# Moving query transposes later in the step and taking extra keys and queries out through the segment's key buffer

## The chip, the cores and the metric

The kernel runs on one core of one Trainium2 chip. The metric is the device time of one execution in microseconds (us), and less is better. The kernel before takes a median of 1097.09 us in three runs (1093.23 to 1100.27). Every run carries the mean clock that was granted to TensorE; a run is called slow when it is over 1.5% above the fastest of the same kernel, and fast otherwise.

## The reference, cut to what matters

The first half is a recurrent attention: 64 segments of 32 tokens each, one after the other, because every segment reads eight memory rows that the segment before it wrote. The second half is a gated feed-forward part; the change does not touch it.

```python
B, S, Dm = (1, 2048, 640);  H, Dh = (32, 128);  M, seg = (8, 32)
for s in range(n_seg):                               # 64 segments, strictly in order
    xs = x[:, s * seg_len:(s + 1) * seg_len, :]
    h = jnp.concatenate([mem, xs], axis=1)           # 8 memory rows + 32 tokens
    q, k, v = h @ Wq, h @ Wk, h @ Wv                 # einsum per head, 32 heads of 128
    p = softmax(mask(q @ k.T * scale))
    o = einsum('bhte,hed->btd', p @ v, Wo)
    mem = o[:, :M, :].copy()                         # the next segment starts from this
    outs.append(o[:, M:, :])
h  = x + concatenate(outs)
h2 = h + feed_forward(layernorm(h))
```

## The kernel before

A **step** is one segment. The columns of a projection that the eight memory rows leave free are used for 24 tokens of later segments, called **riders**. Four steps carry 96 riders; the other 32 tokens of a block of 128 are the **extra** tokens, and they get a projection of their own in three pieces: keys in a third step (`s % 4 == 2`), queries in a fourth step (`s % 4 == 3`), values in the next first step.

A projection lands in PSUM, VectorE and ScalarE cast it into `tok` (four tiles of 128x512, two halves: 0 and 1 for keys, 2 and 3 for queries), and a DMA transpose turns a half into the layout that the scores need. All transposes are issued by SyncE (SP), and the program gives each engine one list of instructions, in the order in which they are recorded. TensorE's part of a step is, in order: the **score block**, the **memory product** (probabilities of the memory rows times the values), the transposing of its result, the **output product**, the **rider product** (`pv_x`), the projections of the next keys and queries, and the **memory pick** (the next memory queries, read straight from `tok`). An **eviction** is the cast of a projection out of PSUM. The helper `add(engine, f, r=, w=)` records an instruction with the keys that it reads and writes, and the waits follow from those keys.

```python
def to_tok(b, t, eng):                               # PSUM bank b -> tok[t]
    copy_op(eng, tok[t][:, :], bank(b), [B(b)], [("tok", t)])

def pick_mem(bk):                                    # L453: memory queries by TensorE, straight from tok
    ...
    add("pe", f, r=[("tok", 2), ("tok", 3), ("ident",)], w=[B(bk)])

def trans_q(after=()):                               # QS <- tok[2,3], DMA transpose, 256 KB
    dma_t(QS[...], tokp[1][:, :], [("tok", 2), ("tok", 3)] + list(after), [("QS",)])

def scores(s):                                       # L572
    ...
    add("pe", f, r=[("KS",), ("Kr", q), ("Qm", q), ("Qr", q)], w=[B(P0), B(P1)])

def extra_units(s):
    ...
    j = (1, 0, 2)[r]                                 # keys, queries, values
    def evac():
        for i, e in enumerate(("act", "act")):
            if j == 2: to_v(BQ[i], Vr[q], i, ("Vr", q), e)
            else:      to_tok(BQ[i], 2 + i, e)       # extra keys and queries: into tok[2,3]
        if j == 1:
            dma_t(Kr[q][...], tokp[1][:, :], [("tok", 2), ("tok", 3)], [("Kr", q)])
    def fin():                                       # extra queries: tok -> QS -> Qr
        trans_q()
        late_q.append(lambda: evac_q(QS, ("QS",), t0, 32, 0, "act"))
    return part, evac, (fin if j == 0 else None)

for s in range(NSEG):
    ...                                              # key projection
    to_tok(BQ[0], 0, "act"); to_tok(BQ[1], 1, "dve")
    dma_t(KS[...], tokp[0][:, :], [("tok", 0), ("tok", 1)], [("KS",)])   # keys of this segment
    trans_ox()
    project(a, ks, 0, (0, 1), (P0, P1), spare=40)    # query projection
    to_tok(P0, 2, "act"); to_tok(P1, 3, "dve")
    for f in late_k + late_q: f()
    qlate = nr and s % 4 < 2
    if nr and not qlate and s < NSEG - 2:
        trans_q()                                    # third and fourth steps: at once
    project(...)                                     # values, first part
    pick_mem(T0)                                     # L453
    ...                                              # values, second part
    scores(s); exp_mem(); exp_x()                    # L572
    if nr:
        v_riders(t0, nr, (), ...)                    # riders' values: Vr <- Vp, plain DMA from POOL
        if s < NSEG - 2 and not qlate:
            evac_q(QS, ("QS",), t0, nr, M, "act")    # QS -> Qr
    ...                                              # extra projection in pieces, memory product (L609)
    if evac: evac()
    wo_pass(T1, ...)                                 # output product (L644)
    ...
    pv_x(s, P0)                                      # rider product (L690)
    if nfin: nfin()
```

The softmax here doesn't subtract the row's maximum and nothing guards it: scores larger than these inputs give would overflow.

## Time and profile before

| | before |
|---|---|
| time, median of 3 | 1097.09 us |
| span and granted clock of the profiled run | 1095.7 us, 0.997 |
| mean step, first / second / third / fourth | 13.39 / 13.64 / 13.51 / 13.47 us |
| TensorE waits for a query eviction at the memory pick | 0.9 us, once |

A step is measured from the start of one score block to the start of the next, over the third to the sixtieth-second segment (15 steps of each kind). What the trace says of the tile QS, of which the last line gives the time from the issue of a transpose into it to its landing:

```profile
DMA to landing us min/median/max: 3.0/3.1/4.9
```

Where QS is transposed early or late in a step, 256 KB take about 3.1 us.

### The profile page before, as it was taken

To read this page: it belongs to the slowest core of one execution; us is meant where nothing else is said; L and a number is where in the kernel's file an instruction comes from. 1 tells how busy PE (TensorE), PEld (TensorE's weight loads), DVE (VectorE), ACT (ScalarE), POOL (GpSimd) and SP (SyncE) were. 2 spreads that over 40 slices of the span, in tenths; PEclk is the share of its full clock that TensorE was granted. 3 is DMA by queue.
4 is the path that set the end of the run, shared out by engine and by line. 5 is a ranking of instruction groups with operands and counts; after the bars stand their busy time and mean duration, and the time that the engine had idled before them with its cause. 6 is when DMAs were issued, how large, how long until landed. Compare 5 with 4: busy or idle time off the path is not lost.

```text
span 1095.7 us, 55782 instructions
## 1 busy us (share of the span) xinstructions
PE 1054.8 (96%) x27875; PEld 517.3 (47%) x23292; DVE 608.8 (56%) x1673; ACT 362.6 (33%) x792; POOL 260.0 (24%) x521
## 2 busy tenths in 40 slices
PE   4689999999999999999999999999999999999999
PEld 2344545454545454544454544454545465444444
DVE  3245656565656565666666666565656554553532
ACT  1214343333333333333333333333333322231211
POOL 1013232323223232323232323232323243000000
PEclk9999999999999999999999999999999999999999
DMA  9946464546454654556566666554555448122100
GB/s 363 387 101 106 89 107 90 102 89 104 90 98 95 102 94 97 94 114 108 112 113 112 110 109 109 100 97 95 95 94 93 92 118 288 45 78 74 29 19 25
DMA packets 285371, 121.61 MB, mean 111 GB/s; under 512 B 260880, under 2 KB 274788, under 8 KB 285136
## 3 DMA queue, kind: packets, MB, share of 16 engines
q1 hardware_dynamic: 267456, 95.52, 41.9%
q0 software_dynamic: 17264, 22.26, 8.8%
q8 instruction: 201, 3.29, 1.3%
q14 instruction: 34, 0.28, 0.1%
q10 hardware_dynamic: 416, 0.26, 0.1%
HBM read 36.79 MB, written 7.19 MB: 40 GB/s over the span
## 4 chain that ended last, share of the span: by engine, by line
PE 91%; DMA 5%; SPq 3%; DVE 1%; issue 1%; ACT 0%; DVEq 0%
PE ps L422 25%; PE ps L400 24%; PE ps L644 13%; PE ps L1051 11%; PE ps L690 3%; PE ps L666 3%; PE ps L572 3%; SPq L360 3%; DMA Wo<-in_A_Wo_dram 3%; PE ps L1092 3%; PE ps L609 2%; DMA KS<-tok 2%; PE ps L453 2%; PE ps L624 1%; DMA Kr<-tok 1%
## 5 line engine op out<-in xcount | busy, mean ns | idle before, releaser
L422 PE MATMUL ps<-W,act_r 128*32 128x512 bf16 x4292 | 406.5, 384 | 6.8 <-DMA W<-in_A_Wv_dram 2.6
L400 PE MATMUL ps<-W,act_r 128*32 128x512 bf16 x3588 | 362.4, 379 | 0.0
L422 PEld LDWEIGHTS ps<-W,act_r 128*32 128x32 bf16 x4292 | 132.1, 97 | 250.4 <-issue 151.3
L360 POOL DMA_DIRECT2D Vr<-Vp x312 | 156.1, 508 | 345.9 <-ACT Px L591 274.0
L464 ACT ACTIVATE tok<-ps 128x512 bf16<-128x512 f32 x192 | 110.9, 593 | 229.0 <-PE ps L400 200.2
L644 PE MATMUL ps<-Wo,oT 128*32 128x160 bf16 x8064 | 156.9, 234 | 8.7 <-DMA Wo<-in_A_Wo_dram 4.8
L466 DVE CAST tok<-ps 128x512 bf16<-128x512 f32 x131 | 90.6, 691 | 129.6 <-PE ps L400 109.8
L644 PEld LDWEIGHTS ps<-Wo,oT 128*32 128x32 bf16 x8064 | 142.8, 97 | 30.3 <-DVE oT L466 16.2
L422 PE MATMUL ps<-W,act_e 128*32 128x512 bf16 x900 | 89.3, 381 | 0.0
L400 PE MATMUL ps<-W,act_e 128*32 128x512 bf16 x900 | 88.9, 379 | 0.0
L555 DVE STREAM_TRANSPOSE TBf<-ps 128x64 f32<-128x64 f32 (+1 forms) x128 | 33.6, 263 | 95.8 <-PE ps L644 95.7
L360 POOL DMA_DIRECT2D attn_d<-wtok x62 | 46.4, 748 | 161.0 <-ACT wtok L464 161.0
L705 DVE TENSOR_TENSOR ox<-ps,rx 128x512 bf16<-128x512 f32 x128 | 82.5, 686 | 2.2
L464 ACT ACTIVATE Qr<-QS 128x512 bf16<-128x512 bf16 (+3 forms) x107 | 69.7, 680 | 35.9 <-DMA QS<-tok 35.9
L464 ACT ACTIVATE Vp<-ps 128x256 bf16<-128x256 f32 (+1 forms) x126 | 48.5, 385 | 81.5 <-PE ps L400 79.0
L1066 DVE TENSOR_TENSOR hT<-g,ps 128x512 bf16<-128x512 bf16 (+1 forms) x56 | 38.5, 688 | 47.2 <-PE ps L1051 43.4
L1051 PE MATMUL ps<-xn2T,Wg 128*128 128x512 bf16 x260 | 64.6, 379 | 0.0
L1051 PE MATMUL ps<-xn2T,Wu 128*128 128x512 bf16 x260 | 64.6, 379 | 0.0
L1064 ACT ACTIVATE g<-ps 128x512 bf16<-128x512 f32 (+1 forms) x56 | 32.4, 592 | 91.6 <-PE ps L1051 91.6
L466 DVE CAST Vp<-ps 128x512 bf16<-128x512 f32 x64 | 44.2, 691 | 28.4 <-PE ps L400 22.9
L464 ACT ACTIVATE wtok<-ps 128x160 bf16<-128x160 f32 x62 | 18.8, 303 | 117.0 <-DVE TBf L555 117.0
L1092 PE MATMUL ps<-Wd,hT 128*128 128x320 bf16 x210 | 57.2, 299 | 0.0
(121 smaller groups left out, 1190.7 us busy)
## 6 DMA issues: line engine op xcount, KB each, us to landing
Vr<-Vp POOLq DMA_DIRECT2D x124, 48.8 KB, 2.0
W<-in_A_Wk_dram SPq DMA_DIRECT2D x2, 2560.0 KB, 13.4
W<-in_A_Wq_dram SPq DMA_DIRECT2D x2, 2560.0 KB, 23.1
W<-in_A_Wv_dram SPq DMA_DIRECT2D x2, 2560.0 KB, 27.7
Wo<-in_A_Wo_dram SPq DMA_DIRECT2D x2, 2560.0 KB, 28.5
xt<-in_A_x_dram SPq DMA_DIRECT2D x30, 160.0 KB, 2.7
Vr<-Vp POOLq DMA_DIRECT2D x96, 32.5 KB, 2.1
at<-attn_d SPq DMA_DIRECT2D x16, 160.0 KB, 3.7
```

The lines of the kernel that those rows point to most:

```text
L360: add(eng, lambda e: e.dma_start(dst, src), r=r, w=w, dma=True)
L400: return pe.add_instruction(mybir.InstMatmult(name=nc.get_next_instruction_name(), engine=mybir.EngineType.PE, ins=[pe.lower_ap(rhs), pe.l ...
L422: ins = pe.matmul(*a, start=(c == 0), stop=(c == DC - 1), skip_group_check=True)
L464: add("act", lambda a: a.activation(dst, src, ACTF.Copy), r=r, w=w)
L466: add("dve", lambda v: v.tensor_copy(dst, src), r=r, w=w)
L555: add("dve", lambda v, lo=lo, hi=hi: v.transpose(TBf[:, lo:hi, :].rearrange("p c t -> p (c t)"), src[:, 32 * lo:32 * hi]), r=[wkey], w=[(" ...
L572: i = pe.matmul(bank((P0, P1)[g % 2])[p:p + (M if a else 32), 40 * k:40 * k + 40], lh, Qr[:, h, q, :], start=True, stop=True, skip_group_c ...
L644: i = pe.matmul(bank(bk)[32 * gg:32 * gg + 32, 0:160], src[:, hb, :], w[:, gg], start=(hb == ORDER[0]), stop=(hb == ORDER[31]), skip_group ...
L705: add("dve", lambda v, kh=kh: v.tensor_tensor(ox[:, :, kh, :], src[:, :, kh, 0:128], ap(rx, kh, [[2, 4], [0, 128]]), ALU.mult), r=[B(b0 + ...
L1051: ins = pe.matmul(bank(bk), w[:, c, lo:lo + 128], xn2T[par][:, :, c, :], start=(c == 0), stop=(c == DC - 1))
L1066: add("dve", lambda v: v.tensor_tensor(hT[par][lo:128, j, :], g1[gi][lo:128, :], bank(bu)[lo:128, :], ALU.mult), r=[B(bu), ("g1", gi)], w= ...
L1092: i = pe.matmul(*a, start=(j == 0), stop=(j == FC - 1), skip_group_check=True)
```

## The change

The intent has two halves. The transpose of the own queries in third and fourth steps was issued just before the scores; moved behind the memory probabilities, it should no longer disturb the instruction fetch of TensorE. And the extra keys and queries, which went through the query half of `tok` and QS, leave through KS, which is idle between the scores and the next segment's keys.

```diff
+    def evac_qx(src, t0):                     # half by VectorE, half by ScalarE: tok -> Qr
+        for n, eng in enumerate(("dve", "act")):
+            for q, o, m, lo in pieces(t0, SEG, 0):
+                copy_op(eng, Qr[:, 16 * n:16 * n + 16, q, ...], src[:, 16 * n:16 * n + 16, lo:lo + m],
+                        [("tok", 2 + n)], [("Qr", q)])
 ... exp_mem:
-                r=[("om",), ("mbd",)], w=[("Pbd", i)])
+                r=[("om",), ("mbd",)], w=[("Pbd", i), ("qgo", i)])
 ... extra_units, evac and fin:
+                elif True:
+                    copy_op(e, KS[...][:, 512 * i:512 * i + 512], bank(BQ[i]), [B(BQ[i])], [("KS",)])
-                dma_t(Kr[q][...], tokp[1][:, :], [("tok", 2), ("tok", 3)], [("Kr", q)])
+                dma_t(Kr[q][...], KS[...], [("KS",)], [("Kr", q)])
-            trans_q()
-            late_q.append(lambda: evac_q(QS, ("QS",), t0, 32, 0, "act"))
+            dma_t(tokp[1][...], KS[...], [("KS",)], [("tok", 2), ("tok", 3)])
+            late_x.append(lambda: evac_qx(tokp[1][...], t0))
 ... loop, after the key evictions (so ahead of the query evictions):
+            for f in late_x:
+                f()
-            if nr and not qlate and s < NSEG - 2:
+            qmid = nr and s % 4 >= 2 and s < NSEG - 2
+            if nr and not qlate and not qmid and s < NSEG - 2:
                 trans_q()
 ... after v_riders:
-                if s < NSEG - 2 and not qlate:
+                if qmid:
+                    trans_q([("qgo", 1)])
+                if s < NSEG - 2 and not qlate and not qmid:
                     evac_q(QS, ("QS",), t0, nr, M, "act")
 ... end of the step:
+            if s > 0 and qmid:
+                late_k.append(lambda t0=t0, nr=nr: evac_q(QS, ("QS",), t0, nr, M, "act"))
```

More of the change, by code (lines that the diff above doesn't have):

```diff
@@ L487, in evac_q @@
             copy_op(eng, Qr[:, :, q, M + o:M + o + m], src[:, :, lo:lo + m], [skey], [("Qr", q)])
+    def evac_qx(src, t0):
+        for n, eng in enumerate(("dve", "act")):
+            for q, o, m, lo in pieces(t0, SEG, 0):
+                copy_op(eng, Qr[:, 16 * n:16 * n + 16, q, M + o:M + o + m], src[:, 16 * n:16 * n + 16, lo:lo + m],
+                        [("tok", 2 + n)], [("Qr", q)])
     def seg_slot(s):
@@ L877, in evac @@
                     to_v(BQ[i], Vr[q], i, ("Vr", q), e)
+                elif True:
+                    copy_op(e, KS[:].rearrange("p h t -> p (h t)")[:, 512 * i:512 * i + 512], bank(BQ[i]), [B(BQ[i])], [("KS",)])
                 else:
@@ L880, in evac @@
             if j == 1:
-                dma_t(Kr[q][:].rearrange("p h t -> p (h t)").rearrange("p (k r) -> p k r", r=128), tokp[1][:, :],
-                      [("tok", 2), ("tok", 3)], [("Kr", q)])
+                dma_t(Kr[q][:].rearrange("p h t -> p (h t)").rearrange("p (k r) -> p k r", r=128),
+                      KS[:].rearrange("p h t -> p (h t)"), [("KS",)], [("Kr", q)])
         def fin():
-            trans_q()
-            late_q.append(lambda: evac_q(QS, ("QS",), t0, 32, 0, "act"))
+            dma_t(tokp[1].rearrange("p (k r) -> p k r", r=128), KS[:].rearrange("p h t -> p (h t)"), [("KS",)],
+                  [("tok", 2), ("tok", 3)])
+            late_x.append(lambda: evac_qx(tokp[1].rearrange("p (h t) -> p h t", t=SEG), t0))
         return part, evac, (fin if j == 0 else None)
@@ L902, in woe_store @@
                 w=[("attne", b, dg)], eng="pool")
-    late, late_q, late_k = [], [], []
+    late, late_q, late_k, late_x = [], [], [], []
     for s in range(NSEG):
@@ L933, in build_kernel @@
             to_tok(BQ[1], 1, "dve")
+            for f in late_x:
+                f()
+            late_x = []
             if last:
```

## The prediction

> **What bounds the kernel now.** I read the page's busy shares first, then the chain that ended last, then TensorE's waits, then the timeline of one group of steps. Two parts of the page and the waits view:
>
> ```profile
> PE 1054.8 (96%) x27875; PEld 517.3 (47%) x23292; DVE 608.8 (56%) x1673; ACT 362.6 (33%) x792; POOL 260.0 (24%) x521
> ...
> PE 91%; DMA 5%; SPq 3%; DVE 1%; issue 1%; ACT 0%; DVEq 0%
> ...
> PE ps L644 <- issue: 2.6, 8, 0.9
> PE ps L572 <- DMA KS<-tok: 1.6, 5, 0.6
> PE ps L453 <- DVE tok L466: 0.9, 1, 0.9
> ```
>
> TensorE is busy 96% of the span and carries 91% of the chain; the DMA and SP-queue shares of the chain are mostly the opening load of weights (until 58 us). Every wait that the view names inside the 64-step loop is small. Only what shortens TensorE's own idle time counts, so I measured each step as the distance between the starts of two score blocks (L572, 64 of them in the trace). Steps come in fours. From the third to the sixtieth the means are 13.39, 13.64, 13.51 and 13.47 us for first, second, third and fourth step, and the cleanest steps take 13.23. Cutting each step at score block, memory product (L609), output product (L644), rider product (L690) and memory pick (L453), and subtracting the near-shortest value of the same piece, leaves an excess of about 18 us in the loop. About 12 us of it lies in third and fourth steps:
> - L644, output product: 6.0 us in third and fourth steps against 1.8 us in first and second.
> - score block to memory product: 2.7 us against 0.2 us (1.57 us in most of these steps, 1.43 in the others).
> - two single stalls, 0.95 and 0.48 us.
>
> The L644 loss looks so in the chain in order of time (start, length, what); a whole block is one line of 128, a broken one is two with nothing named between:
>
> ```profile
> 720.49 2.21 PE ps L644 x128
> ...
> 747.24 1.20 PE ps L644 x66
> 748.44 0.88 issue
> 749.31 1.28 PE ps L644 x62
> ```
>
> TensorE waits for no tile there. The break falls where a 16 KB packet of the instruction queue is due. In the packet records this packet starts a median 1.50 and 1.59 us after the scores in first and second steps, but 1.96 and 2.16 us in third and fourth, where a QS transpose, issued 0.2 to 1.2 us before the scores, is still moving data (its packets come some 1.3 us after the issue). In the worst step it started at 2.46 us, took 1.73 us, and L644 lost 1.11 us.
>
> The SP queue and ScalarE in a third step (scores at 621.28 us):
>
> ```profile
> 620.44 1.23 SPq L363 DMA_TRANSPOSE QS<-tok  x1
> 624.48 0.94 ACT L464 ACTIVATE Qr<-QS 128x512 bf16<-128x512 bf16 x2 [1.26 <-DMA QS<-tok]
> 625.32 1.06 ACT L464 ACTIVATE tok<-ps 128x512 bf16<-128x512 f32 x2
> 626.47 2.25 SPq L363 DMA_TRANSPOSE Kr<-tok  x1
> 629.17 1.21 SPq L363 DMA_TRANSPOSE at<-xt  x1
> 630.71 2.50 SPq L363 DMA_TRANSPOSE KS<-tok  x1
> 633.09 0.60 ACT L464 ACTIVATE tok<-ps 128x512 bf16<-128x512 f32 x1 [2.50 <-DMA Kr<-tok]
> ```
>
> The reader is to see two things: the extra keys leave late, because ScalarE first waits for QS and copies it; and the next queries' eviction waits 2.50 us for the slow Kr transpose, since both use the same half of tok. That became the 0.95 us stall, and it happened once in 15.
>
> **What the Trainium skill says.** "Perfetto Trace Analysis", Identifying the Most-Contended Engine, warns that matmul busy time is no measure of distance to the roofline; so I use step lengths, not the 96%. "Runtime: NRT & Kernel Launch", Instruction fetch mechanics, says instructions come in 16 KiB blocks of 256 over a DMA queue of the sequencer's own, mostly hidden. The trace agrees on the size (three 16,384-byte packets a step) and, in these steps, not on "hidden". "DMA: Bandwidth & Descriptors", Queues, rings and completion order, says each DMA engine changes between queues after each packet. If so a fetch should slip in among the transpose's packets; that it starts 0.5 us later where one is in flight speaks for more delay than that. The same page, Issuing engines are not separate DMA queues, says all issuers share the 16 DMA engines: moving a transpose moves load, it removes none.
>
> **The change part by part.**
> 1. *Own queries of third and fourth steps* (30 transposes): the QS transpose waits for the second half of the memory probabilities, 1.4 to 1.5 us after the scores start instead of 0.2 to 1.2 us before. Its packets then come at about 1.5 + 1.3 = 2.8 us and end near 4.3, after the fetch at 1.4 to 2.4. L644 should then lose what it loses in first and second steps: 6.0 - 1.8 = 4.2 us gained. The delay of the first memory wait, seen with QS in flight and in no first or second step, should go: 2.7 - 0.2 = 2.5 us. Of both I expect some two thirds, as other traffic (riders, stores) stays: 6.7 x 0.65 = 4.4 us.
> 2. *The copy QS to Qr* goes to the next step, behind its first query eviction. ScalarE (33% busy) loses no time on the path; first and second steps work so already, finishing before their scores.
> 3. *Extra keys (third step)* leave PSUM into KS: the same two 0.59 us ScalarE copies, no longer behind QS or tok. Their transposes start about 4.7 us after the scores as in the best steps, not at 5.2, 6.1 and 6.4 as in three of them. The tok wait goes, worth the two single stalls: 1.4 us at most; I take 1.0.
> 4. *The new wait.* KS is also where the next step's keys land, so their transpose must wait until Kr has been read out. Kr is issued at 4.7 and lands in 4.7 to 5.4 us (page: 5.2 median), so at 9.4 to 10.1; the KS transpose is issued at 9.45 today. It lands 3.1 to 3.5 us later and the scores begin at 13.24, so there are about 13.24 - 9.45 - 3.3 = 0.5 us of slack. A mean delay of 0.4 us mostly fits in; I take 0.15 us lost in each of 15 third steps: 2.2 us.
> 5. *Another new wait in the same place*: the attention store issued from the POOL queue at the start of a third step was made to read KS only for ordering; ScalarE must now await its landing before it writes KS. It lands at 3.8 to 4.6 us today and the extra projection ends at 3.4. Without the QS transpose in flight I expect it sooner: the one such store with no QS in flight (near the end of the loop) landed in 2.3 us. So about 3.1 us, no cost; this is the shakiest step.
> 6. *Extra queries (fourth step)* go KS, then tok, then half by VectorE and half by ScalarE into Qr (a 0.3 us and a 0.6 us copy) instead of one 1.05 us ScalarE copy. The transpose from 4.6 lands in 3.7 to 4.2 us, before the KS transpose at 9.45. Off the path: 0.
>
> The compiled TensorE order is the same but for one added wait in the score blocks. Sum: -4.4 - 1.0 + 2.2 = -3.2 us, so about **1094 us**.
>
> **The rivals.**
> - *KS becomes the wait.* If the store still lands at 4.2 us, the key copies end at 5.4, Kr lands at 10.5, KS is issued at 10.6 and lands at 13.9: 0.6 us lost in 14 third steps, 8 us, which eats all gains and gives about 1100 us; with Kr slowed further by QS and riders (they now share 2.8 to 5 us) 1.0 us a step, 1106 us. For it: Kr took 6.6 us once, and KS landings of 4.2 us occur where another transpose was issued just ahead. Against: the slack of 0.5 us.
> - *Fetch delay was not QS.* Second steps lose L644 time too (1.4 us) with no such transpose at that moment. Then only 1.0 us is gained and 2.2 lost: 1098 us.
> - *Everything works.* All 6.7 + 1.4 us gained, no KS wait: 1089 us.
> - *TensorE stays the bound whatever happens.* Even without any loss in third and fourth steps the gain is 12 us, 1.1%; a 2% gain is out of reach, and a 2% loss needs 0.7 us in each of the 30 changed steps.
>
> **Range and chances.** The middle of the working is 1094; the rivals span 1089 to 1106, and the runs of before spread 1093.2 to 1100.3. I take 1085 to 1104. Faster by over 2% 0.01, slower by over 2% 0.02, within 2% 0.97.
>
> **What would show it.** Right if in third and fourth steps the instruction packet starts near 1.5 us and L644 runs unbroken; if ScalarE's waits for QS (35.9 us, 30 times) vanish; if VectorE and ScalarE never wait for Kr before tok; and if the third step's KS transpose is issued by 10 us with TensorE's waits on KS (1.6 us, 5 times) little changed. Wrong if waits of L572 on KS grow to 10 us or more (part 4 or 5), if the key copies start near 4.3 us (part 5), or if the L644 breaks stay (part 1).

## The result, and the profile after

The changed kernel takes a median of **1125.01 us** in four runs (1123.30 to 1128.42); the kernel before took 1095.91 us beside it, also in four. The ratio is **1.0265** (95% interval 1.0222 to 1.0309). A ratio here is always the mean time of one kernel's fast runs over the mean of the other's fast runs of the same rounds, so it is not quite the quotient of the medians. The prediction had put 0.02 on such an outcome.

Lines moved by six in the middle of the file: the scores are now L578, the memory product L615, the output product L650, the rider product L696. The page's busy shares and chain of the kernel after:

```profile
PE 1061.9 (95%) x27875; PEld 521.0 (46%) x23292; DVE 612.4 (55%) x1688; ACT 357.4 (32%) x792; POOL 260.1 (23%) x521
...
PE 81%; DMA 12%; SPq 3%; DVE 2%; issue 1%; ACT 1%; DVEq 0%
```

TensorE has the same number of instructions and is busy 95% of the span, so the first line shows hardly anything. The second does: TensorE's share of the chain fell from 91% to 81%, and DMA's rose from 5% to 12%. TensorE's own waits and the queue's waits (engine, line, what was waited for: us in total, times, longest) say where:

```profile
PE ps L453 <- DVE tok L466: 21.2, 14, 3.3
...
PE ps L422 <- issue: 3.8, 10, 0.8
...
PE ps L578 <- DMA KS<-tok: 2.1, 5, 0.7
```

```profile
SPq L166 <- DMA QS<-tok: 54.7, 15, 4.4
...
SPq L166 <- DMA tok<-KS: 42.8, 14, 4.2
```

The wait for KS, which the prediction had feared most, is still small. The memory pick of L453 waits 21.2 us for the query eviction, 14 times; before it was 0.9 us, once. Fourteen times in 15 blocks of four is a per-block effect. The steps show which:

| mean us of a piece | score block to memory product | to transposing its result | to output product | output product | rider product to pick | pick to next scores | step |
|---|---|---|---|---|---|---|---|
| third, before | 1.55 | 1.24 | 0.57 | 2.45 | 6.08 | 1.63 | 13.51 |
| third, after | 1.43 | 1.24 | 0.57 | 2.33 | 6.22 | 1.70 | 13.48 |
| fourth, before | 1.49 | 1.24 | 0.57 | 2.61 | 5.96 | 1.60 | 13.47 |
| fourth, after | 1.42 | 1.24 | 0.57 | 2.33 | 7.62 | 1.86 | 15.03 |

Times 15, the fourth steps cost 23.4 us more, third steps 0.4 us less, first steps 0.2 us less and second steps 1.4 us more. The profiled spans differ by 25.9 us; nearly all of the rest lies in the second segment, which is 1.6 us longer (14.73 us against 13.11). That is not the change's: the trace after has an interval of half clock there, at 72 us, and the trace before has none; of the runs below, third_only and no_riders4 have such an interval too and take 14.85 and 14.73 us, fourth_only has none there and takes 13.21. Within the fourth steps the parts that the change aimed at did get shorter (1.1 and 4.3 us), and the stretch from the rider product to the pick got 24.9 us longer.

Here is one fourth step of the kernel after (scores at 428.64, the next at 443.39), the chain in order of time: start, length, what.

```profile
430.24 5.20 DMA QS<-tok
...
435.50 4.45 DMA tok<-KS
...
439.98 0.30 DVE Qr L466
...
440.31 0.64 ACT Qr L464
...
441.04 0.70 DVE tok L466
441.74 0.05 issue
441.79 0.36 PE ps L453 x8
```

Five links follow each other without a gap. The own queries' transpose, issued 1.60 us after the scores, reads `tok[2,3]`. The extra queries' transpose *writes* `tok[2,3]` and so cannot be issued before the first has landed. Its result must be copied out of `tok` before the next queries can be cast into it. VectorE copies first, then ScalarE (both write the same key of Qr), and only then may VectorE cast the queries into the tile that ScalarE has just read. The memory pick ends the chain. The same step in the timelines of SP, POOL and VectorE:

```profile
430.24 1.53 SPq L363 DMA_TRANSPOSE QS<-tok  x1
435.50 1.23 SPq L363 DMA_TRANSPOSE tok<-KS  x1
440.03 1.23 SPq L363 DMA_TRANSPOSE KS<-tok  x1
```

```profile
430.55 2.00 POOL L360 DMA_DIRECT2D Vr<-Vp  x4 [1.25 <-ACT Px L597]
```

```profile
439.98 0.29 DVE L466 COPY Qr<-tok 128x512 bf16<-128x512 bf16 x1 [2.06 <-DMA tok<-KS]
441.04 0.69 DVE L466 CAST tok<-ps 128x512 bf16<-128x512 f32 x1 [0.77 <-ACT Qr L464]
```

The reader is to see the POOL line: the rider stores are issued from 0.3 us after the QS transpose on, and QS takes 5.2 us instead of 3.1. The tile view of QS, whose last line before read 3.0/3.1/4.9, has a new maximum; its median hides the matter because first and second steps are unchanged:

```profile
DMA to landing us min/median/max: 3.1/3.1/6.5
```

Over the 15 fourth steps `tok<-KS` is issued a median 6.66 us after the scores (5.30 to 8.38). The key transpose of the next segment, which shares the SP queue, moves with it, from a median 9.58 to 11.39 us.

One small part of the loss is of another kind. The granted clock of the profiled run is 0.989 against 0.997, and all four runs after have 0.988 to 0.992. From the third to the sixty-second segment the trace has three intervals of 3.4 us at half clock (332, 554 and 670 us), each within 1 us after one of the long waits at L453; the trace before has none there. The Trainium skill, "TensorE: Matmul & The Clock Gate", Part 1: The HAM clock gate, gives the idle state half the clock and a window of about 3.4 us, and the trace agrees with both figures. If all work in these intervals ran at half speed they cost at most 3 x 1.7 = 5 us (an estimate), already contained in the step lengths above. They come after the waits, and they are not the main loss: the trace of fourth_only below has only one of them and the same long fourth steps (14.96 us).

### The profile page after: what moved, and what is told of

Same layout as the page of the kernel before. It is cut to its first block, busy times and chain, and to the rows that moved or that the text cites. A ratio compares the mean times of both kernels' runs of the same rounds, so it can differ in the third digit from the quotient of the medians.

```text
span 1121.6 us, 55749 instructions
## 1 busy us (share of the span) xinstructions
PE 1061.9 (95%) x27875; PEld 521.0 (46%) x23292; DVE 612.4 (55%) x1688; ACT 357.4 (32%) x792; POOL 260.1 (23%) x521
## 4 chain that ended last, share of the span: by engine, by line
PE 81%; DMA 12%; SPq 3%; DVE 2%; issue 1%; ACT 1%; DVEq 0%
PE ps L422 22%; PE ps L400 20%; PE ps L650 12%; PE ps L1068 10%; DMA tok<-KS 5%; PE ps L672 3%; PE ps L578 3%; PE ps L696 3%; SPq L360 3%; DMA Wo<-in_A_Wo_dram 3%; PE ps L1109 3%; DMA QS<-tok 2%; PE ps L615 2%; DMA KS<-tok 2%; PE ps L453 2%; PE ps L630 1%
## 5 line engine op out<-in xcount | busy, mean ns | idle before, releaser
L422 PE MATMUL ps<-W,act_r 128*32 128x512 bf16 x4292 | 413.2, 387 | 9.2 <-issue 3.8
L400 PE MATMUL ps<-W,act_r 128*32 128x512 bf16 x3588 | 366.3, 381 | 0.0
L650 PE MATMUL ps<-Wo,oT 128*32 128x160 bf16 x8064 | 156.3, 236 | 4.2 <-DMA Wo<-in_A_Wo_dram 3.1
L650 PEld LDWEIGHTS ps<-Wo,oT 128*32 128x32 bf16 x8064 | 144.9, 98 | 22.9 <-DVE oT L466 16.8
L464 ACT ACTIVATE tok<-ps 128x512 bf16<-128x512 f32 x132 | 78.3, 593 | 201.1 <-PE ps L400 176.5
L400 PE MATMUL ps<-Wd,hT 128*128 128x320 bf16 x210 | 57.2, 299 | 0.0
L1109 PE MATMUL ps<-Wd,hT 128*128 128x320 bf16 x210 | 57.2, 299 | 0.0
```

The lines of the kernel that those rows point to most:

```text
L400: return pe.add_instruction(mybir.InstMatmult(name=nc.get_next_instruction_name(), engine=mybir.EngineType.PE, ins=[pe.lower_ap(rhs), pe.l ...
L422: ins = pe.matmul(*a, start=(c == 0), stop=(c == DC - 1), skip_group_check=True)
L464: add("act", lambda a: a.activation(dst, src, ACTF.Copy), r=r, w=w)
L650: i = pe.matmul(bank(bk)[32 * gg:32 * gg + 32, 0:160], src[:, hb, :], w[:, gg], start=(hb == ORDER[0]), stop=(hb == ORDER[31]), skip_group ...
L1109: i = pe.matmul(*a, start=(j == 0), stop=(j == FC - 1), skip_group_check=True)
```

## The experiments

The theory after the first look: fourth steps lose because the query half of `tok` is still tied up when the next queries arrive. It needs three things together: **(a)** the extra queries are transposed into the tile that the late QS transpose still reads, **(b)** that transpose is slowed by the rider stores, **(c)** the copies stand ahead of the query evictions. The rivals: the loss comes from KS and the third steps (the prediction's own rival), or merely from later transposes sharing DMA with more traffic. Twelve kernels were run in five batches. Ratios are against the kernel before in the same batch. Labels of edits are relative to the kernel after.

### One half of the change at a time

**third_only** keeps the third step's half; **fourth_only** the fourth step's; **own_early4** keeps all of the change but leaves the own queries' transpose of fourth steps at its old place.

```diff
 third_only
-                elif True:
+                elif j == 1:
-            dma_t(tokp[1][...], KS[...], ...); late_x.append(...)
+            trans_q()
+            late_q.append(lambda: evac_q(QS, ("QS",), t0, 32, 0, "act"))
-            qmid = nr and s % 4 >= 2 and s < NSEG - 2
+            qmid = nr and s % 4 == 2 and s < NSEG - 2
 fourth_only
-                elif True:
+                elif j == 0:
-                      KS[...], [("KS",)], [("Kr", q)])
+                      tokp[1][:, :], [("tok", 2), ("tok", 3)], [("Kr", q)])
-            qmid = nr and s % 4 >= 2 and s < NSEG - 2
+            qmid = nr and s % 4 == 3 and s < NSEG - 2
 own_early4
-            if nr and not qlate and not qmid and s < NSEG - 2:
+            if nr and not qlate and s < NSEG - 2 and (not qmid or s % 4 == 3):
-                if qmid:
+                if qmid and s % 4 != 3:
```

> Only the third step's parts of the change: its own queries late, its extra keys through KS; the fourth step as in the kernel before. Theory (the whole loss is in the fourth step): third steps about 13.5 us, fourth 13.5 us, time 1093 to 1098 us, the same as before. Rival (the keys' buffer KS, with the store that reads it, is the wait): 1108 us or more.

> Only the fourth step's parts; the third step as in the kernel before. Theory: the loss is all here, 1118 to 1126 us, TensorE waits at L453 about 20 us. Rival (the two steps' parts need one another, or the third carries it): under 1108 us.

> The changed kernel, but in fourth steps alone the own queries' QS transpose starts at its old place (before the scores); the extra queries still go KS, tok, Qr. Theory (the late QS transpose holds the tok half, so the extra queries' transpose starts at 6.5 to 8.4 us instead of 4.6): tok<-KS is issued near 4.7 us after the scores and lands by 9.5, TensorE's waits at L453 fall from 21.2 us to under 4, the fourth step falls from 15.0 to about 13.5 us, time about 1101 us. Rival (the detour through KS and tok is itself too long, or VectorE's place in its queue): fourth step stays over 14.3 us, time over 1112 us.

Measured, against 1097.78 us before: third_only 1094.78 us, ratio 0.9996 (0.9952 to 1.0040); fourth_only 1123.22 us, 1.0233 (1.0192 to 1.0275); own_early4 1097.13 us, 1.0003 (0.9981 to 1.0024). The wait at the memory pick in their traces, in this order:

```profile
PE ps L453 <- DVE tok L466: 0.9, 1, 0.9
```

```profile
PE ps L453 <- DVE tok L466: 22.2, 14, 3.2
```

```profile
PE ps L453 <- DVE tok L466: 0.3, 1, 0.3
```

The loss and the wait are in the fourth step's half alone. The rival of the prediction, a loss through KS in third steps, falls: third_only has the new KS route for the keys and costs nothing. And own_early4 narrows it further. It still takes the extra queries by KS and `tok`, with the same copies ahead of the evictions; only the own queries' transpose is early again. One step of it (scores at 417.19) has the extra transpose issued 4.78 us after the scores:

```profile
416.71 1.26 SPq L363 DMA_TRANSPOSE QS<-tok  x1
421.97 1.24 SPq L363 DMA_TRANSPOSE tok<-KS  x1
```

So neither the KS detour nor the copies hurt by themselves. The later QS transpose does; that it does so through `tok` is shown by own_buffer below.

### The rider stores

**no_riders4** leaves the rider stores out in fourth steps. That gives wrong values; the comparison with the reference was within tolerance all the same, so it is no proof of correctness. **riders_after4** keeps them but lets them wait until QS has landed.

```diff
 no_riders4
-                v_riders(t0, nr, (), ...)
+                if s % 4 != 3:
+                    v_riders(t0, nr, (), ...)
 riders_after4
-                v_riders(t0, nr, (), ...)
-                if qmid:
+                if qmid and s % 4 == 3:
+                    trans_q([("qgo", 1)])
+                v_riders(t0, nr, [("QS",)] if qmid and s % 4 == 3 else (), ...)
+                if qmid and s % 4 != 3:
                     trans_q([("qgo", 1)])
```

> The changed kernel without the rider stores Vr<-Vp of fourth steps (wrong values on purpose). If those stores slow the QS transpose: it lands in about 3.2 us (at 4.8 after the scores) instead of 4.9 to 5.8, tok<-KS is issued near 4.9, fourth step about 13.5 us, time about 1101 us. If they do not: QS lands as late as now, tok<-KS at 6.5 or later, time 1118 us or more.

> The changed kernel, but in fourth steps the rider stores wait until the QS transpose has landed; all values right. Theory (riders beside QS are what makes it late): QS lands in 3.3 us, tok<-KS is issued near 4.8 but now shares with the riders and lands in 4 to 5 us, at 9 to 9.8; fourth step 13.3 to 13.9 us, time 1094 to 1105 us. Rival (the extra transpose, now beside the riders, is slowed as QS was): fourth step over 14.3 us, over 1112 us.

Measured: no_riders4 1096.28 us, 0.9992 (0.9957 to 1.0028), against 1097.78. QS lands in about 3.3 us. One step (scores at 416.13) on SP:

```profile
417.73 1.23 SPq L363 DMA_TRANSPOSE QS<-tok  x1
420.87 1.70 SPq L363 DMA_TRANSPOSE tok<-KS  x1
...
425.43 1.23 SPq L363 DMA_TRANSPOSE KS<-tok  x1
```

QS is issued 1.60 us after the scores exactly as in the kernel after, and yet the next transpose follows 3.14 us later instead of 5.26. That is link (b). (The edit also shortens the second transpose, from a median 4.2 to 3.1 us in the four landings that each trace has; riders_after4 below relieves QS alone.) The fourth step falls to 13.16 us, 0.31 below before: this is what the change's gain looks like undisturbed. Part of it returns elsewhere: the scores wait for KS 7.4 us, 11 times, most of it (4.5 us) at the end of third steps, which are the same code as in the kernel after but 13.74 us long here.

riders_after4: 1104.29 us against 1098.15, 1.0040 (0.9997 to 1.0082). QS lands in 3.45 us and `tok<-KS` is issued at 4.75 us, both as wanted, but now the riders meet the second transpose, which takes a median 5.25 us instead of 4.2 (four landings each):

```profile
PE ps L453 <- DVE tok L466: 6.8, 9, 1.6
```

Two thirds of the wait are gone and one third stays: the traffic was moved, not removed.

### A buffer of their own for the extra queries

There were 1564 free bytes per partition. A 2 KB buffer XS fits if it shares 512 bytes with a tile that is used in second steps only. **own_buffer** lets the extra queries go KS -> XS -> Qr, with the copies where they were; **own_buffer_late** also puts the copies behind the query evictions.

```diff
 own_buffer
+    XS = ar.alloc("XS", [128, H, SEG], BF16)      # its last 512 bytes are oTn's
-            dma_t(tokp[1][...], KS[...], [("KS",)], [("tok", 2), ("tok", 3)])
-            late_x.append(lambda: evac_qx(tokp[1][...], t0))
+            dma_t(XS[...], KS[...], [("KS",)], [("oTn",)])
+            late_x.append(lambda: evac_qx(XS, t0))
 own_buffer_late, further
-            for f in late_x:
-                f()
-            late_x = []
-            for f in late_k + late_q:
+            for f in late_x + late_k + late_q:
```

> The changed kernel, but the extra queries' transpose writes a buffer of its own (XS, sharing 512 bytes with oTn, which no fourth step uses) instead of the tok half; QS still starts late and the riders still slow it. Theory (it is the wait for tok, behind the slowed QS, that costs): XS<-KS is issued near 4.7 us, fourth step 13.3 to 13.7 us, time 1093 to 1102 us. Rival (the late, slowed QS delays whatever follows it in the DMA queues, tok or not): XS lands after 10 us, fourth step over 14.2 us, time over 1110 us.

> As own_buffer, and the two copies XS to Qr stand behind the next queries' evictions instead of ahead of them. If part of the loss is the place in VectorE's and ScalarE's queues: a few tenths of a us less in the fourth step than own_buffer, 1092 to 1098 us. If the place costs nothing once XS lands by 9.4 us: equal to own_buffer within 0.3%. If ScalarE now fills up before the scores: the first step 0.2 to 0.4 us longer, 3 to 6 us more.

Measured against 1098.15: own_buffer 1099.69 us, 1.0017 (0.9985 to 1.0049); own_buffer_late 1097.67 us, 1.0001 (0.9968 to 1.0034). Both traces have no wait at the pick worth naming. QS is as late as in the kernel after and slower still (6.4 to 8.5 us in the three landings that each trace has), and the rider stores are all there; only the collision on `tok` is gone, and with it the whole loss. That settles link (a). Link (c) is worth little once (a) is gone: the two fourth steps are 13.54 and 13.53 us long.

But own_buffer_late should have been *faster* than before, since the output product is whole (2.33 us) and nothing waits. The gain went into the next piece: rider product to pick takes 6.34 us in fourth steps against 5.96 before, and TensorE's waits show an unnamed one inside the projections:

```profile
PE ps L423 <- issue: 3.8, 9, 1.1
```

In the packet records the second 16 KB instruction packet of these steps starts a mean 6.02 us after the scores, 0.46 us after the rider product starts. Before it started at 5.91 us, but there the rider product starts later too, at the same 5.91 us. Over the 15 fourth steps of this run, the packet's start correlates at 0.95, its end at 0.97, with the length of the piece from rider product to pick. It looks as if, in place of the first packet of the step, the second is now delayed.

### Is it the traffic at the second packet?

**both_own_buffer** takes the extra keys through XS as well. **buffer_no_riders** is own_buffer_late without rider stores in third and fourth steps (wrong values). **buffer_riders_after** is own_buffer_late with the riders behind QS in fourth steps.

```diff
 both_own_buffer
-                    copy_op(e, KS[...], bank(BQ[i]), [B(BQ[i])], [("KS",)])
+                    d, k = (XS, "oTn") if j == 1 else (KS, "KS")
+                    copy_op(e, d[...], bank(BQ[i]), [B(BQ[i])], [(k,)])
-                      KS[...], [("KS",)], [("Kr", q)])
+                      XS[...], [("oTn",)], [("Kr", q)])
 buffer_no_riders
-                v_riders(t0, nr, (), ...)
+                if s % 4 < 2:
+                    v_riders(t0, nr, (), ...)
 buffer_riders_after: as riders_after4
```

> As own_buffer_late, and the third step's extra keys are also staged in XS, so neither the next keys' transpose nor the attention store holds them. Theory: nothing of the change's new waits is left and its gains at L644 (about 6 us) and at the first memory wait (about 2 us) remain: third steps 13.3, fourth 13.2 to 13.4 us, 1087 to 1093 us, faster than both kernels by 0.4 to 0.8% over before. Rival (the gains return as waits elsewhere): 1095 us or more.

> own_buffer_late without the rider stores of third and fourth steps (wrong values on purpose). Question: own_buffer_late takes the tok wait away and L650 stays unbroken, yet it only equals the kernel before; its rider-product-to-pick piece is 0.10 us longer in third and 0.38 us longer in fourth steps than in the kernel before, with the second instruction packet late. Theory (QS, slowed by the riders, is now beside that second packet): the packet starts by 5.2 us on average, that piece is 5.93 to 6.0 us in both steps, third steps about 13.3 and fourth about 13.2 us, time 1085 to 1092 us. Rival (the extra transposes themselves delay the packet): the piece stays over 6.15 us, time 1094 us or more.

> own_buffer_late, and in fourth steps the riders wait until QS has landed (right values): a try at a version that beats both kernels. Theory: fourth steps lose the second-packet delay, 13.2 to 13.35 us instead of 13.53, time 1090 to 1095 us, 0.2 to 0.6% under the kernel before. Rival (the riders now stand beside the extra queries' transpose and delay it or the next keys): fourth step 13.5 us or more, 1097 us or more, nothing won.

both_own_buffer: 1099.81 us against 1098.15, 1.0021 (0.9995 to 1.0047). This missed what I expected of it (1087 to 1093). Its fourth step is better (13.25), but its third step, where the keys are now issued without waiting for the store, is worse: 13.70 us, with 6.51 us from rider product to pick. The unnamed wait grew rather than went:

```profile
PE ps L423 <- issue: 5.2, 11, 0.9
```

buffer_no_riders: 1090.78 us against 1100.41, **0.9901** (0.9867 to 0.9935). Third and fourth steps are 13.18 and 13.12 us long, the piece is 5.94 and 5.93, the second packet starts at a mean 5.26 us in fourth steps, and the unnamed wait is down to

```profile
PE ps L423 <- issue: 1.6, 5, 0.5
```

This is the only kernel that beat the one before clear of noise, by 1%, and it does so by leaving out work. It shows that, with the tile collision gone, the rest of the expected gain is held back where rider stores and transposes move together. That they do it by delaying the instruction packet is what the packet starts (6.02 against 5.26) and the correlation suggest; no run held up a packet by anything else.

buffer_riders_after: 1099.10 us against 1100.41, 1.0006 (0.9974 to 1.0037). The piece is 5.93 us and the packet starts at 5.27 us, as without riders. But XS<-KS, now beside the riders, lands at a median 9.86 us (four landings), and the key transpose may not write KS before KS has been read out. It is issued at a median 10.46 us instead of 9.30 in own_buffer_late. This is the prediction's rival "KS becomes the wait", only in the fourth step. The queue's wait and TensorE's:

```profile
SPq L166 <- DMA XS<-KS: 48.3, 14, 4.0
```

```profile
PE ps L579 <- DMA KS<-tok: 9.4, 16, 1.3
```

In own_buffer_late the queue waited so for 18.9 us, 5 times. From pick to scores the fourth step takes 2.19 us instead of 1.63. The traffic came back as another wait and nothing was won.

### The copies, and a second way to hold tok

**uncrossed** asks how much of the loss is the crossing of the copies: ScalarE casts the next queries into `tok[2]` and VectorE into `tok[3]`, but VectorE copies out of 2 and ScalarE out of 3, one after the other. The edit gives each engine the tile that it fills next, and a key of Qr of its own. The copies also name their tile of `tok` as written, which keeps the following cast behind them.

```diff
-        for n, eng in enumerate(("dve", "act")):
+        for n, eng in enumerate(("act", "dve")):
-                        [("tok", 2 + n)], [("Qr", q)])
+                        [("tok", 2 + n)], [(("Qr", "Qx")[n], q), ("tok", 2 + n)])
 scores:
-        add("pe", f, r=[("KS",), ("Kr", q), ("Qm", q), ("Qr", q)], ...)
+        add("pe", f, r=[("KS",), ("Kr", q), ("Qm", q), ("Qr", q), ("Qx", q)], ...)
```

> The changed kernel, but each engine copies out the quarter of tok that it fills next, and the two copies no longer wait for one another: in the changed kernel VectorE's 0.29 us copy, ScalarE's 0.63 us copy and VectorE's 0.69 us eviction follow one another, 1.8 us from landing to pick; here the longer of 0.63 + 0.60 and 0.29 + 0.69, about 1.3 us. Theory (the rest of the loss is the late landing): fourth steps 0.5 us shorter, about 14.5 us, time 1114 to 1119 us. Rival (the copies' order is what costs): under 1106 us. Rival (it hides under something else): 1122 us or more.

Its four runs are 1124.61 (slow state), 1105.14, 1116.25 and 1117.35 us; the three fast ones give 1.0160 (1.0101 to 1.0220) against 1095.89 before, with the verdict "unclear". Against the 1.0265 of the kernel after this suggests some 11 us saved of 29 ((1.0265 - 1.0160) x 1096), but the runs scatter by 12 us and were not taken in the same rounds as the kernel after. It is a hint that link (c) takes a share as long as (a) stands, no more.

**own_queries_last** was meant as a version that wins: own_buffer_late, with the own queries' transpose of fourth steps issued behind the extra queries' one, out of the way of both packets.

```diff
-                if qmid:
+                if qmid and s % 4 != 3:
                     trans_q([("qgo", 1)])
 ... end of the step:
+        if s > 0 and qmid and s % 4 == 3:
+            trans_q()
```

> own_buffer_late, and in fourth steps the own queries' transpose is issued behind the extra queries' one (about 6.0 us after the scores), clear of the riders and, by its packets, of the first two instruction packets; all values right. Theory: QS lands in 3 to 4 us, by 10 us and before the next query eviction at 10.9; L650 2.33 us, the next piece 5.95 us, fourth step 13.15 to 13.3 us instead of 13.53, time 0.3 to 0.6% under the kernel before. Rival (it now meets the next keys' transpose at 9.3 us): the pick-to-scores piece grows over 1.8 us and nothing is won.

It missed badly: 1119.24 us in the median of six runs against 1092.73. One of the six was slow; the five fast ones give 1.0203 (1.0172 to 1.0235). One step of it (scores at 427.96, the next at 443.19), its wait at the pick, and VectorE's wait before the query eviction:

```profile
432.70 1.88 SPq L364 DMA_TRANSPOSE XS<-KS  x1
434.62 1.31 SPq L364 DMA_TRANSPOSE QS<-tok  x1
...
437.26 1.24 SPq L364 DMA_TRANSPOSE KS<-tok  x1
```

```profile
PE ps L454 <- DVE tok L467: 23.2, 14, 2.3
```

```profile
DVE tok L467 <- DMA QS<-tok: 40.1, 14, 3.8
```

QS is issued a median 6.66 us after the scores, and behind XS it needs 5.5 us (median of the three landings in the trace, 3.7 to 6.0), so it lets go of `tok` at about 12.1 us; the next query eviction wants the tile at about 10.9. No extra queries pass through `tok` here and no copy stands in front, and yet it is the same wait, as often and as long as in the kernel after. That is the strongest form of the result: the loss is whatever still holds `tok[2,3]` when the next queries come.

All fourth steps together (mean us; issue times are medians after the scores):

| kernel | tok released by | output product | rider product to pick | pick to scores | step |
|---|---|---|---|---|---|
| before | QS<-tok of the extra queries, issued at 6.22 | 2.61 | 5.96 | 1.60 | 13.47 |
| after | copies of tok<-KS, issued at 6.66 | 2.33 | 7.62 | 1.86 | 15.03 |
| own_early4 | copies of tok<-KS, issued at 4.79 | 2.49 | 5.98 | 1.62 | 13.33 |
| no_riders4 | copies of tok<-KS, issued at 4.74 | 2.33 | 5.97 | 1.64 | 13.16 |
| riders_after4 | copies of tok<-KS, issued at 4.75, slower | 2.33 | 6.43 | 1.64 | 13.65 |
| own_buffer_late | QS<-tok, issued at 1.60 | 2.33 | 6.34 | 1.63 | 13.53 |
| buffer_no_riders | QS<-tok, issued at 1.60 | 2.33 | 5.93 | 1.63 | 13.12 |
| own_queries_last | QS<-tok, issued at 6.66 | 2.35 | 7.54 | 1.74 | 14.86 |

The first row shows that a late issue is not enough. Before, the extra queries' transpose was issued almost as late as the one after, but it landed by 9.3 us in the four landings that the trace has, and nothing had to be copied out of `tok` behind it.

## Why the prediction was wrong

The prediction said 1094 us, within 2%; the result is 1125.01, slower by 2.65%. Point by point:

- **What bounds the kernel:** right. TensorE's idle time was the thing to count, and the loss is TensorE's idle time at one line.
- **Part 1, own queries later: it came as the prediction said.** The first packet of fourth steps now starts at a mean 1.54 us instead of 2.08 and the output product is one unbroken line, as in this fourth step's chain; with the transpose put back (own_early4) the packet starts at 2.13 us again and the product takes 2.49 us instead of 2.33:

```profile
600.99 2.24 PE ps L650 x128
```

  Output products gained 6.0 us in the 30 steps and the first memory wait 2.9, where 4.4 had been taken for both. What the step did not say is that the transfers stay somewhere: in third steps, 2.1 us of it returned between rider product and pick, and own_buffer_late shows that fourth steps would have returned 5.7 us (15 x 0.38) there even without the collision.
- **Part 2, the copy of QS to Qr in the next step:** nothing in any run speaks against it; no run tested it alone.
- **Part 3, the wait of evictions for Kr is gone:** right, it is in no list of waits after.
- **Part 4, KS must be read out before the next keys:** about right. 2.2 us were allowed. The third steps' key transpose is issued at a median 9.97 us instead of 9.61, and pick to scores grew by 1.0 us in total. TensorE's waits for KS went from 1.6 to 2.1 us, five times in both. But the size was lucky: the third step of third_only, own_early4 and no_riders4 is the same, and there pick to scores takes 1.65, 1.83 and 2.01 us instead of 1.63 before, so 0.3 to 5.7 us in 15 steps. The prediction had also taken 9.45 us for the issue before, near the earliest of the 15.
- **Part 5, the store is out of the way by 3.1 us: wrong, and harmless.** It landed at 3.3 to 4.6 us, and ScalarE stood waiting for it:

```profile
ACT KS L464 <- DMA attn_d<-at: 26.5, 13, 2.6
```

  The prediction had called this the shakiest step and had built its main rival on it. ScalarE is not on the path there, and third_only shows that it costs nothing measurable.
- **Part 6, extra queries "Off the path: 0": this is the step that failed.** It took the transpose "from 4.6", landing before the keys need the queue at 9.45. Measured are a median 6.66 us for the issue and 10.3 to 12.4 for the landing (four in the trace), and 24.9 us (to the pick) plus 3.8 us (on to the scores) lost in 15 fourth steps. The numbers for the copies were right (0.29 and 0.63 us). What was missing is a dependency and its size: part 1 had just placed a *reader* of `tok[2,3]` at 1.5 us and part 6 placed a *writer* of the same tile at 4.6, and the two were never put on one time line. Even on it, "1.5 + 3.1 = 4.6" would have looked safe; it needed also that the riders, issued in the same moment, stretch the 3.1 us to about 5.1 (riders_after4 takes this away and two thirds of the wait with it; no_riders4 takes away the slowing of both transposes and the whole wait). Nor was 4.6 us what the trace before mostly showed: 8 of its 15 extra transposes were issued at 6.2 to 7.2 us. The prediction had written that QS and riders share the stretch from 2.8 to 5 us, but only as a cost to Kr.
- **The rivals:** "KS becomes the wait" looked in the third step, and the loss came in the fourth at another tile. "A 2% loss needs 0.7 us in each of the 30 changed steps" was correct arithmetic that was taken for a safeguard; the loss came as 1.56 us in each of 15.

What stays open: how much of the loss the half-clock intervals make (at most 5 us, an estimate; the trace of fourth_only has one of them and loses as much in each fourth step), and the exact share of the copies' crossing, since uncrossed gave no readable profile. Why a packet of instructions is held up by transposes and stores in flight is not shown either, only that it is later with them and on time without.

## What to carry to other kernels

When one change moves a reader of a buffer later and another adds a writer of the same buffer, draw both on one time line, with the durations they will have beside the traffic of their *new* place, not those of the old one. A buffer is free when its last reader is done, so moving a transfer that nobody waits for can still delay everything that reuses its source. And moving traffic away from one sensitive moment only helps if there is an insensitive one to move it to: three of the experiments above (riders_after4, both_own_buffer, buffer_riders_after) turned one wait into another.

## What the Trainium skill lacked or had wrong

- "DMA: Bandwidth & Descriptors", Latency and other measured facts, gives an effective bandwidth of 261 GB/s for one DMA-transpose pattern, which would be 1.0 us for 256 KB (an estimate from that figure). In these traces a 256 KB transpose between SBUF tiles takes 3.1 us from issue to landing when undisturbed. The figure is a bandwidth and the 3.1 us include the start (the first packets come some 1.3 us after the issue) and the end of a transfer, so the two do not contradict each other; what is missing is a time to landing for a transpose.
- No page says how much a transpose slows when small stores from another queue start with it: in fourth steps 3.1 to 3.3 us (no_riders4) became about 5 us (after: 4.9 to 5.8 where the landing is in the trace), beside four rider stores issued within 2 us.
- "Runtime: NRT & Kernel Launch", Instruction fetch mechanics, calls the cost of a fetch mostly hidden. Here the same move of a transpose made the output product 0.28 us shorter in each fourth step (2.61 to 2.33), and taking the rider stores away shortened the piece at the next packet by 0.41 us in each fourth step (6.34 to 5.93). That the packet is what links them is suggested by its starts and not shown.
- "TensorE: Matmul & The Clock Gate", Part 1: The HAM clock gate, has the idle state follow at least one idle window of about 3.4 us. Here it came after less: waits of 2.0, 2.7 and 3.3 us inside a loop that is otherwise busy were each followed by 3.4 us at half clock, while another wait of 2.0 us (at 218 us) was not.
